# Lead of a fused attention and two-layer MLP kernel: load order, and value-block means by products with value rows as weights

## The chip, the cores and the metric

The kernel runs on one core of one Trainium2 chip. The metric is the device time of one execution in microseconds (us); lower is better. Before the change the median of three runs is 583.91 us (583.61 to 584.04).

## The reference, cut to what matters

Attention over a window of neighbours and over 24 block summaries of 32 positions each (maximum of the keys, mean of the values), then two MLP layers on the 1,536 tokens.

```python
# q, k, v: (B, H, S, D) = (2, 8, 768, 64); block, window = 32, 16; nb = S // block = 24
k_sum = k.reshape(B, H, nb, block, D).max(axis=3)
v_sum = v.reshape(B, H, nb, block, D).mean(axis=3)
scores_l = scale * np.matmul(q, k.transpose(0, 1, 3, 2))          # kept where |i - j| < window
scores_s = scale * np.einsum('bhsd,bhnd->bhsn', q, k_sum) + np.log(block)
a = softmax(concatenate([where(mask_l, scores_l, -1e9), scores_s], -1))
x = matmul(a, concatenate([v, v_sum], axis=2))                    # -> (1536, 512)
h = np.maximum(x @ w_in, 0.0);  x = h * h @ w_out                 # 512 -> 2048 -> 512
h = x @ w_in2;  out = (h * sigmoid(h)) @ w_out2
```

What the change touches is `v_sum` of the first of the two batches, and the order in which the first inputs are fetched.

## The kernel before

**Tiles.** The queries are cut into 24 tiles of 64 positions, 12 per batch. A tile sees 96 keys of its window and 24 block summaries, 120 columns in all. The eight heads are taken as four pairs (`NHP`, "pair 0" to "pair 3"). The first eight tiles are called the lead (`NLEAD`): their attention must be done before the first MLP product can start. The MLP works on blocks of 512 tokens, the first of which is just these eight tiles. TensorE products of the MLP are in fp32r, split into a high and a low part; the products of the attention are in plain fp32.

**Steps of the lead.** The functions inside `first_block` (lines 635 to 840) are named as the planner names them:

- `kt`, `q`, `cst`, `vr`, `vl` (lines 663 to 681) issue loads on SyncE's queue (SP): a pair's keys (384 KB), the queries of four lead tiles (512 KB), mask and identity matrix (244 KB), 256 value rows (512 KB), and the 96 value rows of each of four tiles (768 KB). In the profile these are `t_ksum`, `qrlead`, `cst_sb`, `vrows` and `vlead`.
- `ksum` (VectorE, line 684) takes the maximum over each block of 32 keys; `kwl` (ScalarE, 691) and `ksl` (VectorE, 696) copy windows and maxima of a pair into `kws`, 120 columns for each of four tiles.
- `psl(g, hp)` (TensorE, 698 to 707) makes the scores of tile g for head pair hp: two products of 64 by 64 by 120 (`pss`, four records in the trace). Behind psl(3, 0) and psl(3, 1) it also issues 6 and 4 idle products of 512 columns (`turn`, `FILL`, line 47), which keep TensorE busy; ten more stand at the very start (`WARM`, line 650).
- `ttl` (VectorE, 437) adds the mask and takes the row minimum, `exl` (ScalarE, 444) the exponential; `ze`, `rc`, `nt` (VectorE, 464 to 477) the guard, the inverse and the scaling by it. In the trace these have tile `T` (and `m`, `z`, `r`).
- `psa(g)` (TensorE, 479) transposes a tile's weights, four transposes; `a(g)` (485) copies them out of PSUM, on ScalarE for tiles 0 to 4, on VectorE for tiles 5 to 7.
- `vs(c)` (TensorE, 709 to 711) adds 128 value rows to the 24 block means in `psv`: one fp32 product of 512 columns, with a window of `share` as weights, into rows 96 to 119 of one PSUM bank. `share` holds 1/32 in four of its 88 columns, and the window slides by four with c. The six `vs` accumulate.
- `vmean(i)` (ScalarE, 713) copies the means out of PSUM into the last 24 rows of `vlead`, for four tiles at once.
- `av(g)` (TensorE, 810) multiplies the weights of tiles g and g+1 with `vlead`; `xh` (ScalarE) and `xl` (VectorE) split the result into the high and low part of `xt`, the input of the MLP.
- `sc`, `sh`, `st2`, `hi`, `lo` (753 to 770) decode and split a chunk of MLP weights: `sc` and `hi` on ScalarE, the others on VectorE.
- `highs(0)` (772) is the first MLP product; it needs all four `xh`. `gemm10` adds the low part of the input, `gemm11` is the next chunk.

```python
        def vs(c):
            lo = NSUM - P // KBLK - c * (P // KBLK)
            mm(psv[NWIN:NK], share[:, lo:lo + NSUM], vrows[c // 2][:, c % 2], start=(c == 0), stop=(c == S // P - 1))
```

**What sets the order.** `first_order()` (lines 70 to 241) is a planner in Python. Each step has an engine, a duration, a due time and the steps it waits for; the planner places them one after another, always the step that can start first on its engine, among those ready by then the one due first. Loads are taken to land one after another at a fixed rate. The result is a fixed sequence, and SP, TensorE, ScalarE and VectorE each execute their steps in exactly that order (`manual_schedule`, line 890). A step that waits holds back everything behind it on its engine. PSUM tiles are shared: all four `psl` of a tile write one bank, and its four `ttl` read it; a step that touches a bank waits for the steps of other engines that touch it and stand ahead of it in the sequence.

Of the kernel before, what the change touches and what calls it, by code (L numbers as in the profile page):

```python
# [10 lines left out]
F32 = mybir.dt.float32  # L11
# [8 lines left out]
B, H, S, D = 2, 8, 768, 64  # L20
# [49 lines left out]
def first_order():  # L70
# [6 lines left out]
    def op(eng, name, arg, dur, due, deps=(), bank=(), kb=0):  # L77
        o = index[name, arg] = dict(eng=eng, name=name, arg=arg, dur=dur, due=due + shift.get(name, 0), deps=list(deps), bank=bank, kb=kb,
                                    n=len(ops))
        ops.append(o)  # L80
# [17 lines left out]
        return 24 + 7 * s  # L98


    for i, (name, arg, kb) in enumerate([("kt", 0, 393), ("q", 0, 524), ("kt", 1, 393), ("cst", 0, 250), ("kt", 2, 393),
                                         ("kt", 3, 393), ("q", 1, 524), ("vr", 0, 524), ("vr", 1, 524), ("vr", 2, 524),
                                         ("vl", 0, 1150), ("vl", 1, 1150)]):
        load(name, arg, kb, -100 + i)
    for hp in range(NHP):
        op("vec", "ksum", hp, 1.0, -50 + hp, [("kt", hp, 0)])
# [1 line left out]
            op("act", "kwl", (hp, i), .5, -50 + hp + 51 * i, [("kt", hp, 0)])  # L108
            op("vec", "ksl", (hp, i), .13, -50 + hp + 48 * i, [("ksum", hp, 0)])
    for c in range(6):  # L110
        op("pe", "vs", c, .92, 2.7 + .1 * c, [("vr", c // 2, 0)])
    for i in range(NLEAD // NGRP):
        op("act", "vmean", i, 1.9, -5, [("vs", c, M) for c in range(6)] + [("vl", i, 0)] * 0)
    for i in range(NVF):
        op("act", "vfm", i, .6, tile_due(NLEAD) - 10 + i, [("vmean", 0, 0), ("xh", LEADX[-1], 0)])

# [10 lines left out]
    for g in range(NFIRST):  # L127
        due, two = tile_due(g), g - 2 >= NLEAD
        if g < NLEAD:
            for hp in range(NHP):  # L130
                op("pe", "psl", (g, hp), .29, due, [("kwl", (hp, g // NGRP), A), ("ksl", (hp, g // NGRP), A), ("q", g // NGRP, 0)] +
                   [("psl", (g, hp - 1), 0)] * (hp > 0), bank=[] if hp else [("acc", "ttl", (g, NHP - 1))])
                op("vec", "ttl", (g, hp), .21, due, [("psl", (g, hp), M), ("cst", 0, 0)])
                op("act", "exl", (g, hp), .385, due, [("ttl", (g, hp), A)])
            exp = [("exl", (g, hp), A) for hp in range(NHP)]
        else:
            load("kw", g, 246, due - 9, [pss(g - 2) + (M,)] * two)
            load("qr", g, 131, due - 8.9, [("qd", g - 2, A)] * two)
            load("vf", g, 196, due - 6, [av(g - 2) + (M,)] * two)
            op("vec", "kwc", g, .13, due - .5, [("kw", g, 0)] + [("kvr", 2 * NHP - 1, 0)] * (g >= TPB))  # L140
            if TPB <= g < TPB + NVF:
                op("vec", "vfc", g, .35, due, [("vf", g, 0), ("vendc", 0, A)])
            op("pool", "qd", g, .72, due - 5, [("qr", g, .1)] + [pss(g - 2) + (M,)] * two)
            if g == NLEAD:
                op("pe", "vis", g, 1.95, due, [("gemm1", 1, 0), ("kwc", g, A), ("qd", g, A)], bank=[("att", "ttr", g, g + 1)])
            elif g % 2 == 0:
                op("pe", "vis", g, 3.1, due, values(g - 2) + values(g - 1) + [("kwc", g, A), ("qd", g, A)],
                   bank=[("h", "xl", g - 2), ("att", "ttr", g, g + 1)])
            else:
                index["vis", g - 1]["deps"] += [("kwc", g, A), ("qd", g, A)]  # L150
            op("vec", "ttr", g, .84, due, [pss(g) + (M,)] + [psa(g - 2) + (M,)] * two)
            op("act", "exp", g, 1.54, due, [("ttr", g, -.45)])
            exp = [("exp", g, A)]
        op("vec", "ze", g, .09, due, exp)
        op("vec", "rc", g, .1, due, [("ze", g, .1)])
        op("vec", "nt", g, .78, due, [("rc", g, .1)])
        if g < NLEAD:
            op("pe", "psa", g, .62, due - 2, [("nt", g, -.1)], bank=[("att", "a", g)])
        elif g % 2 == 0:
            op("pe", "psa", g, .85, due - 2, [("nt", g, -.1)], bank=[("att", "a", g, g + 1)])  # L160
        else:
            index["psa", g - 1]["deps"] += [("nt", g, -.1)]
        op("vec" if g in AVEC else "act", "a", g, .65 if g in AVEC else .56, due, [psa(g) + (M,)] + [av(g - 2) + (M,)] * (g >= NLEAD + 2))
        if g < NLEAD and g % 2:
            op("pe", "av", g - 1, 1.15, due, [("vl", g // NGRP, 0), ("vmean", g // NGRP, A), ("a", g - 1, A), ("a", g, A)],
               bank=[("acc", "xl", g - 1)])
            op("act", "xh", g - 1, .6, due, [("av", g - 1, M)])
            op("vec", "xl", g - 1, .7, due, [("xh", g - 1, A)])
        elif g % 2:
            if g == NFIRST - 1:  # L170
                op("pe", "av", g - 1, 1.3, due, values(g - 1) + values(g), bank=[("h", "xl", g - 1)])
            op("act", "xh", g - 1, .6, due, [av(g) + (M - 1.8 * (g < NFIRST - 1),)])
            op("vec", "xl", g - 1, .7, due, [("xh", g - 1, A)])
# [71 lines left out]
def kernel(  # L245
# [32 lines left out]
    def mm(o, l, r, **kw):  # L278
        pe.matmul(o, l, r, **kw)  # L279

    def copy(eng, o, i, scale=1.0):
        if eng is act:
            return act.activation(out=o, in_=i, func=AF.Copy, scale=scale)  # L283
        return eng.tensor_copy(out=o, in_=i)  # L284
# [88 lines left out]


    share_p = ctx.enter_context(tc.tile_pool(name="share_p", bufs=1, side="right"))
    share = share_p.tile([P, PHASE - 8], F32, tag="share", name="share")
    att_ctx = ExitStack()
    cp = att_ctx.enter_context(tc.tile_pool(name="cp", bufs=1, side="right"))
    p1 = att_ctx.enter_context(tc.tile_pool(name="p1", bufs=1, side="right"))
# [14 lines left out]

    pool.memset(share, 0.0)
    for j in range(P // KBLK):
        pool.memset(share[j * KBLK:(j + 1) * KBLK, NSUM - P // KBLK + j:NSUM - P // KBLK + j + 1], 1.0 / KBLK)
    st = {}

    def summaries(b, sums, tag):  # L400
# [234 lines left out]
    def first_block():  # L635
# [3 lines left out]

        idle_in = wi_p.tile([P, 512], F32R, tag="wi", name="idle_in")  # L640
        idle_out = ps_h.tile([P, 512], F32, tag="h", name="idle_out")
        psv = ps_h.tile([P, DM], F32, tag="h", name="psv0")
        vec.memset(idle_in.bitcast(F32), 0.0)
        early = first_p.tile([P, 1], F32, tag="early", name="early")
        act.activation(out=early, in_=idle_in[:, 0:1].bitcast(F32), func=AF.Exp)
# [18 lines left out]
            sp.dma_start(out=kts[hp][:, WIN:], in_=kT[0, hp])  # L664

        def q(i):
            gr = slice(i * NGRP, i * NGRP + NGRP)
            sp.dma_start(out=qrlead[i], in_=qW[gr].rearrange("g e d n -> (e d) g n"))

        def cst_(_):  # L670
            sp.dma_start(out=cst_sb[:, 0:3 * NK + P], in_=cst)
# [35 lines left out]
            turn(FILL.get(ghp, 0))  # L707

        def vs(c):
            lo = NSUM - P // KBLK - c * (P // KBLK)  # L710
            mm(psv[NWIN:NK], share[:, lo:lo + NSUM], vrows[c // 2][:, c % 2], start=(c == 0), stop=(c == S // P - 1))

        def vmean(i):
            means = psv[NWIN:NK]
            copy(act, vlead[NWIN:NK, i * NGRP:i * NGRP + NGRP].rearrange("p g h d -> p g (h d)"),
                 bass.AP(means.tensor, means.offset, [means.ap[0], [0, NGRP], means.ap[1]]))

# [101 lines left out]
        def psa(g):  # L819
            for i in (g,) if g < NLEAD else (g, g + 1):  # L820
                transposes(i)

        do = dict(kt=kt, q=q, cst=cst_, vr=vr, vl=vl, ksum=ksum_, kwl=kwl, ksl=ksl, vs=vs, vmean=vmean, vfm=vfm, kv=kv, kvr=kvr,
                  vend=vend, vendc=vendc, vfc=vfc, kw=kw_load, qr=q_load, vf=v_load, kwc=k_sums, qd=side_by_side,
                  vis=vis, ttr=minima, exp=exps, ze=guard, rc=inverse, psl=psl, ttl=lambda a: minimum(*a),
                  exl=lambda a: exponential(*a), nt=lambda g: norm(g, vec),
# [393 lines left out]
```

## Time and profile before

| what | us |
|---|---|
| median of three runs | 583.91 (583.61 to 584.04) |
| the profiled execution: its own time | 583.73 |
| the profiled execution: its span | 581.9 |
| TensorE busy in the span | 574.5 |
| VectorE busy | 386.4 |
| ScalarE busy | 360.1 |
| start of the first MLP product (highs) | 34.91 |

The span runs from the first to the last instruction; the execution's own time includes what lies around it. PE is TensorE's products, PEld its weight loads, DVE is VectorE, ACT is ScalarE, SPq the issue of loads. Most TensorE products go through the helper `mm` and so stand at line 279, copies at 283 and 284: the tile's name tells them apart. An fp32 product appears as two records, each with a weight load of its own.

### The profile page before, as it was taken

What the parts mean: (1) busy time and instruction counts of PE and PEld (TensorE: products, weight loads), DVE (VectorE), ACT (ScalarE), POOL (GpSimd) and SP (SyncE); (2) the same over time, 40 slices, a digit from 0 to 9 for tenths busy, and PEclk for the clock granted to TensorE, in tenths of its full rate; (3) what the DMA queues carried; (4) which work ended last, traced back from release to release, by engine and by line L of the source; (5) the groups of instructions that cost most, each with busy time, mean ns of one, the idle gap of its engine ahead of it and who ended that gap; (6) DMA issues with size and microseconds to landing.
All of it is one profiled execution on the core that took longest, in us unless ns stands there. A gap on an engine that the chain in (4) does not pass through costs nothing.

```text
span 581.9 us, 9507 instructions
## 1 busy us (share of the span) xinstructions
PE 574.5 (99%) x3300; PEld 489.5 (84%) x3300; DVE 386.4 (66%) x966; ACT 360.1 (62%) x834; POOL 93.0 (16%) x101
## 2 busy tenths in 40 slices
PE   8999999999999999999999999999999999999997
PEld 6578888888888888888888889999988988889995
DVE  5999899953955765286454778666665666666641
ACT  5999878864646545376544677565555655555541
POOL 0010100102654452175332200000000000000000
PEclk9999999999999999999999999999999999999999
DMA  8999989755998879345880111242258411111002
GB/s 317 310 267 330 316 296 333 241 212 168 295 339 289 298 245 364 122 134 160 313 262 2 38 54 73 90 146 90 91 169 338 146 37 37 36 37 37 27 12 108
DMA packets 42240, 104.42 MB, mean 179 GB/s; under 512 B 4560, under 2 KB 11856, under 8 KB 42192
## 3 DMA queue, kind: packets, MB, share of 16 engines
q1 hardware_dynamic: 42192, 103.81, 52.7%
q8 instruction: 26, 0.43, 0.3%
q14 instruction: 22, 0.18, 0.1%
HBM read 78.37 MB, written 25.43 MB: 178 GB/s over the span
## 4 chain that ended last, share of the span: by engine, by line
PE 96%; ACT 2%; DMA 1%; DVE 1%; SPq 0%; issue 0%; DVEq 0%
PE acc L279 45%; PE h L279 23%; PE hx L279 12%; PE hz L279 6%; PE pss L279 3%; PE hy L279 3%; PE psa L483 2%; PE av L279 1%; DMA t_ksum<-in_kT_dram 1%; PE psv L279 1%; ACT vlead L283 1%; ACT T L446 0%; ACT xt L283 0%; PE idle_out L279 0%; DVE ksum L684 0%; DVE T L441 0%
## 5 line engine op out<-in xcount | busy, mean ns | idle before, releaser
L279 PE MATMUL h<-xt,wi 128*128 128x512 f32 x576 | 139.8, 392 | 1.0 <-ACT xt L283 1.0
L279 PE MATMUL acc<-g,wo 128*128 128x512 f32 x576 | 139.5, 391 | 0.0
L279 PE MATMUL acc<-wq,g 128*128 128x512 f32 x576 | 134.3, 390 | 0.0
L279 PEld LDWEIGHTS h<-xt,wi 128*128 128x128 f32 x576 | 107.1, 188 | 23.9 <-ACT xt L283 1.1
L279 PEld LDWEIGHTS acc<-g,wo 128*128 128x128 f32 x576 | 107.6, 188 | 22.6 <-issue 0.5
L279 PEld LDWEIGHTS acc<-wq,g 128*128 128x128 f32 x576 | 107.8, 188 | 21.9 <-DVE wq L287 0.3
L287 DVE TENSOR_TENSOR g<-r,g 128x512 fp32r<-128x512 f32 x48 | 38.8, 807 | 66.0 <-ACT g L283 40.1
L287 DVE TENSOR_TENSOR r_s<-v,r_s 128x256 fp32r<-128x256 f32 x48 | 20.3, 426 | 64.7 <-ACT r_s L283 64.7
L283 ACT ACTIVATE e<-hx 128x384 f32<-128x384 f32 x32 | 15.7, 492 | 60.4 <-PE hx L279 60.4
L446 ACT ACTIVATE T<-T,m 128x120 f32<-128x120 f32 x96 | 36.6, 382 | 7.0 <-DVE m L441 6.9
L283 ACT ACTIVATE g<-s 128x384 fp32r<-128x384 f32 x64 | 32.9, 516 | 10.5 <-DVE s L287 10.4
L279 PE MATMUL hx<-x_t,r_s 128*128 128x384 f32 x192 | 38.5, 335 | 0.0
L287 DVE TENSOR_TENSOR g<-s,g 128x384 fp32r<-128x384 f32 x64 | 35.3, 555 | 2.7 <-ACT g L283 1.1
L279 PEld LDWEIGHTS hx<-x_t,r_s 128*128 128x128 f32 x192 | 33.8, 188 | 0.3
L1032 ACT ACTIVATE s<-e 128x384 f32<-128x384 f32 x48 | 25.1, 523 | 8.4 <-DVE e L287 7.1
L284 POOL COPY qd<-qr 128x256 f32<-128x256 f32 x16 | 12.0, 767 | 111.0 <-PE pss L279 68.2
L287 POOL TENSOR_TENSOR wo<-c_wo,wo 128x512 fp32r<-128x512 f32 x16 | 25.9, 1619 | 19.2 <-ACT wo L283 18.7
L588 ACT ACTIVATE r<-h 128x512 f32<-128x512 f32 x16 | 9.6, 597 | 30.9 <-PE h L279 30.9
L592 ACT ACTIVATE r<-h 128x512 f32<-128x512 f32 x16 | 9.5, 593 | 30.6 <-PE h L279 30.6
L287 DVE TENSOR_TENSOR s<-e,s 128x384 f32<-128x384 f32 x48 | 26.4, 551 | 0.3 <-ACT s L1032 0.3
L287 POOL TENSOR_TENSOR r<-r 128x512 f32<-128x512 f32 x16 | 16.6, 1040 | 49.3 <-ACT g L593 38.1
L477 DVE TENSOR_SCALAR T<-T,r 128x120 f32<-128x120 f32 x96 | 24.2, 316 | 0.5
(112 smaller groups left out, 905.8 us busy)
## 6 DMA issues: line engine op xcount, KB each, us to landing
raw_wi<-in_w_in_dram SPq DMA_DIRECT2D x16, 512.0 KB, 5.0
raw_wo<-in_w_out_dram SPq DMA_DIRECT2D x16, 512.0 KB, 5.4
raw_wp<-in_w_out_dram SPq DMA_DIRECT2D x16, 512.0 KB, 4.9
split<-wo SPq DMA_DIRECT2D x16, 512.0 KB, 3.8
raw_wj<-in_w_in_dram SPq DMA_DIRECT2D x16, 512.0 KB, 4.7
wo<-split SPq DMA_DIRECT2D x16, 512.0 KB, 3.6
c<-scr_dram SPq DMA_DIRECT2D x32, 256.0 KB, 2.8
scr_dram<-c_wo SPq DMA_DIRECT2D x16, 256.0 KB, 3.7
```

The source lines that it names most:

```text
L279: pe.matmul(o, l, r, **kw)
L283: return act.activation(out=o, in_=i, func=AF.Copy, scale=scale)
L284: return eng.tensor_copy(out=o, in_=i)
L287: return eng.tensor_tensor(out=o, in0=a, in1=b, op=op)
L446: act.activation(out=d["T"][:, c], in_=d["T"][:, c], func=AF.Exp, bias=d["m"][:, c:c + 1], scale=-1.0, accum_out=d["z"][:, c:c + 1])
L477: st["norm"] = vec.tensor_scalar(out=T[:, c], in0=T[:, c], scalar1=r[:, c:c + 1], scalar2=None, op0=ALU.mult)
L483: pe.transpose(ps[0:NK, c], d["T"][:, c], id_sb)
L588: act.activation(out=r, in_=h, func=AF.Relu)
L592: act.activation(out=r, in_=h, func=AF.Relu)
L1032: act.activation(out=s, in_=src, func=AF.Sigmoid)
```

## The change

- The loads are reordered: mask and identity become the third load. The queries come in four loads of two tiles (256 KB each) instead of two of four tiles; `psl(g, hp)` waits for load `g // 2`. The last query load stands behind the first MLP weight chunk, which the planner now places ahead of both `vl`.
- `share` keeps only four columns (1/32 where row block and column agree). `vs(c)` is now four fp32 products: 128 value rows by 128 channels as weights, `share`'s four columns as the moving operand. Each yields four block means, channels on the partitions, in its own columns of `psv`; nothing is accumulated.
- `vsc` (VectorE) copies these 96 columns to `vsumT`, and `vst` (TensorE) turns them with four fp32 products, `vsumT` as weights and the identity as moving operand, so that the means stand in rows 96 to 119 as before. `vmean` reads that tile.
- The planner gets new durations and due times for these steps, and so a new order for the whole lead.

```diff
--- before.py
+++ after.py
@@ -98,9 +98,9 @@
         return 24 + 7 * s
 
 
-    for i, (name, arg, kb) in enumerate([("kt", 0, 393), ("q", 0, 524), ("kt", 1, 393), ("cst", 0, 250), ("kt", 2, 393),
-                                         ("kt", 3, 393), ("q", 1, 524), ("vr", 0, 524), ("vr", 1, 524), ("vr", 2, 524),
-                                         ("vl", 0, 1150), ("vl", 1, 1150)]):
+    for i, (name, arg, kb) in enumerate([("kt", 0, 393), ("q", 0, 262), ("cst", 0, 250), ("kt", 1, 393), ("q", 1, 262),
+                                         ("kt", 2, 393), ("kt", 3, 393), ("q", 2, 262), ("vr", 0, 524), ("vr", 1, 524),
+                                         ("vr", 2, 524), ("q", 3, 262), ("vl", 0, 1150), ("vl", 1, 1150)]):
         load(name, arg, kb, -100 + i)
     for hp in range(NHP):
         op("vec", "ksum", hp, 1.0, -50 + hp, [("kt", hp, 0)])
@@ -108,9 +108,11 @@
             op("act", "kwl", (hp, i), .5, -50 + hp + 51 * i, [("kt", hp, 0)])
             op("vec", "ksl", (hp, i), .13, -50 + hp + 48 * i, [("ksum", hp, 0)])
     for c in range(6):
-        op("pe", "vs", c, .92, 2.7 + .1 * c, [("vr", c // 2, 0)])
-    for i in range(NLEAD // NGRP):
-        op("act", "vmean", i, 1.9, -5, [("vs", c, M) for c in range(6)] + [("vl", i, 0)] * 0)
+        op("pe", "vs", c, .47, 1.4 + .1 * c, [("vr", c // 2, 0)])
+    op("vec", "vsc", 0, .3, 1.4, [("vs", c, M) for c in range(6)])
+    op("pe", "vst", 0, .9, -4, [("vsc", 0, A)])
+    op("act", "vmean", 0, 1.9, 1.4, [("vst", 0, M)])
+    op("act", "vmean", 1, 1.9, 1.9, [("vst", 0, M)])
     for i in range(NVF):
         op("act", "vfm", i, .6, tile_due(NLEAD) - 10 + i, [("vmean", 0, 0), ("xh", LEADX[-1], 0)])
 
@@ -128,7 +130,7 @@
         due, two = tile_due(g), g - 2 >= NLEAD
         if g < NLEAD:
             for hp in range(NHP):
-                op("pe", "psl", (g, hp), .29, due, [("kwl", (hp, g // NGRP), A), ("ksl", (hp, g // NGRP), A), ("q", g // NGRP, 0)] +
+                op("pe", "psl", (g, hp), .29, due, [("kwl", (hp, g // NGRP), A), ("ksl", (hp, g // NGRP), A), ("q", g // 2, 0)] +
                    [("psl", (g, hp - 1), 0)] * (hp > 0), bank=[] if hp else [("acc", "ttl", (g, NHP - 1))])
                 op("vec", "ttl", (g, hp), .21, due, [("psl", (g, hp), M), ("cst", 0, 0)])
                 op("act", "exl", (g, hp), .385, due, [("ttl", (g, hp), A)])
@@ -373,7 +375,7 @@
 
 
     share_p = ctx.enter_context(tc.tile_pool(name="share_p", bufs=1, side="right"))
-    share = share_p.tile([P, PHASE - 8], F32, tag="share", name="share")
+    share = share_p.tile([P, PHASE - 8], F32, tag="share", name="share")[:, 0:P // KBLK]
     att_ctx = ExitStack()
     cp = att_ctx.enter_context(tc.tile_pool(name="cp", bufs=1, side="right"))
     p1 = att_ctx.enter_context(tc.tile_pool(name="p1", bufs=1, side="right"))
@@ -394,7 +396,7 @@
 
     pool.memset(share, 0.0)
     for j in range(P // KBLK):
-        pool.memset(share[j * KBLK:(j + 1) * KBLK, NSUM - P // KBLK + j:NSUM - P // KBLK + j + 1], 1.0 / KBLK)
+        pool.memset(share[j * KBLK:(j + 1) * KBLK, j:j + 1], 1.0 / KBLK)
     st = {}
 
     def summaries(b, sums, tag):
@@ -639,7 +641,7 @@
 
         idle_in = wi_p.tile([P, 512], F32R, tag="wi", name="idle_in")
         idle_out = ps_h.tile([P, 512], F32, tag="h", name="idle_out")
-        psv = ps_h.tile([P, DM], F32, tag="h", name="psv0")
+        psv = ps_h.tile([P, NHP, NSUM], F32, tag="h", name="psv0")
         vec.memset(idle_in.bitcast(F32), 0.0)
         early = first_p.tile([P, 1], F32, tag="early", name="early")
         act.activation(out=early, in_=idle_in[:, 0:1].bitcast(F32), func=AF.Exp)
@@ -664,8 +666,8 @@
             sp.dma_start(out=kts[hp][:, WIN:], in_=kT[0, hp])
 
         def q(i):
-            gr = slice(i * NGRP, i * NGRP + NGRP)
-            sp.dma_start(out=qrlead[i], in_=qW[gr].rearrange("g e d n -> (e d) g n"))
+            lo = 2 * i % NGRP
+            sp.dma_start(out=qrlead[2 * i // NGRP][:, lo:lo + 2], in_=qW[2 * i:2 * i + 2].rearrange("g e d n -> (e d) g n"))
 
         def cst_(_):
             sp.dma_start(out=cst_sb[:, 0:3 * NK + P], in_=cst)
@@ -707,11 +709,21 @@
             turn(FILL.get(ghp, 0))
 
         def vs(c):
-            lo = NSUM - P // KBLK - c * (P // KBLK)
-            mm(psv[NWIN:NK], share[:, lo:lo + NSUM], vrows[c // 2][:, c % 2], start=(c == 0), stop=(c == S // P - 1))
+            n = P // KBLK
+            for hp in range(NHP):
+                mm(psv[:, hp, c * n:(c + 1) * n], vrows[c // 2][:, c % 2, hp * P:(hp + 1) * P], share, start=True, stop=True)
+
+        def vsc(_):
+            vsumT[0] = first_p.tile([P, NHP, NSUM], F32, tag="vsumT0", name="vsumT0")
+            copy(vec, vsumT[0], psv)
+
+        def vst(_):
+            ps = st["vst"] = ps_h.tile([P, NHP, P], F32, tag="h", name="pst0")
+            for hp in range(NHP):
+                mm(ps[NWIN:NK, hp], vsumT[0][:, hp], id_sb, start=True, stop=True)
 
         def vmean(i):
-            means = psv[NWIN:NK]
+            means = st["vst"][NWIN:NK].rearrange("p c d -> p (c d)")
             copy(act, vlead[NWIN:NK, i * NGRP:i * NGRP + NGRP].rearrange("p g h d -> p g (h d)"),
                  bass.AP(means.tensor, means.offset, [means.ap[0], [0, NGRP], means.ap[1]]))
 
@@ -820,7 +832,7 @@
             for i in (g,) if g < NLEAD else (g, g + 1):
                 transposes(i)
 
-        do = dict(kt=kt, q=q, cst=cst_, vr=vr, vl=vl, ksum=ksum_, kwl=kwl, ksl=ksl, vs=vs, vmean=vmean, vfm=vfm, kv=kv, kvr=kvr,
+        do = dict(kt=kt, q=q, cst=cst_, vr=vr, vl=vl, ksum=ksum_, kwl=kwl, ksl=ksl, vs=vs, vsc=vsc, vst=vst, vmean=vmean, vfm=vfm, kv=kv, kvr=kvr,
                   vend=vend, vendc=vendc, vfc=vfc, kw=kw_load, qr=q_load, vf=v_load, kwc=k_sums, qd=side_by_side,
                   vis=vis, ttr=minima, exp=exps, ze=guard, rc=inverse, psl=psl, ttl=lambda a: minimum(*a),
                   exl=lambda a: exponential(*a), nt=lambda g: norm(g, vec),
```

## Rows read from the trace of the kernel before

**Rows 1.** The page, busy time by engine: us (share of the span) xinstructions.

```profile
PE 574.5 (99%) x3300; PEld 489.5 (84%) x3300; DVE 386.4 (66%) x966; ACT 360.1 (62%) x834; POOL 93.0 (16%) x101
```

**Rows 2.** Time by stretches: length, busy us of each engine, granted clock, DMA share, GB/s.

```profile
11.83:27.93 16.10, 15.93 (x133) 9.81 (x133) 15.41 (x103) 15.04 (x64) 0.00 (x0) 1.00 1.05 315
27.93:34.91 6.98, 5.42 (x138) 4.77 (x137) 5.73 (x16) 6.85 (x9) 1.27 (x2) 1.00 0.99 301
34.91:581.90 546.99, 543.16 (x2980) 467.85 (x2980) 359.54 (x829) 332.03 (x745) 90.77 (x86) 1.00 0.50 171
```

**Rows 3.** Chain of waits in order of time: start us, us, what.

```profile
17.93 0.91 PE pss L279 x12
...
20.92 0.43 PE pss L279 x4
21.35 1.83 PE psv L279 x4
23.18 0.58 PE psa L483 x4
...
25.31 2.70 PE psv L279 x6
...
33.86 0.51 ACT wi L283
...
34.91 5.74 PE h L279 x24
```

**Rows 4.** Timeline of ScalarE: start us, us, instruction [idle before it <-releaser].

```profile
27.29 0.38 ACT L446 ACTIVATE T<-T,m 128x120 f32<-128x120 f32 x1
...
28.04 3.63 ACT L283 ACTIVATE vlead<-psv 24x2048 f32<-24x2048 f32 x2 [0.28 <-PE psv L279]
```

**Rows 5.** Timeline of SP's queue: issue us, us, instruction.

```profile
1.18 0.42 SPq L668 DMA_DIRECT2D qrlead<-in_qW_dram  x1
...
2.19 0.43 SPq L671 DMA_DIRECT2D cst_sb<-in_cst_dram  x1
```

**Rows 6.** Loads issued from 1.15 and from 2.17 us: KB each, us to landing.

```profile
qrlead<-in_qW_dram SPq DMA_DIRECT2D x1, 512.0 KB, 4.1
...
cst_sb<-in_cst_dram SPq DMA_DIRECT2D x1, 244.0 KB, 6.0
```

**Rows 7.** Timeline of VectorE.

```profile
8.74 0.28 DVE L441 CUSTOM_DVE_ANT_0 T<-pss,cst_sb 128x120 f32<-128x120 f32 x1
...
9.71 0.28 DVE L441 CUSTOM_DVE_ANT_0 T<-pss,cst_sb 128x120 f32<-128x120 f32 x1 [0.28 <-PE pss L279]
...
12.33 0.21 DVE L284 COPY kws<-ksum 128x96 f32<-128x96 f32 x1
12.46 0.28 DVE L441 CUSTOM_DVE_ANT_0 T<-pss,cst_sb 128x120 f32<-128x120 f32 x1
```

**Rows 8.** Timeline of TensorE's products.

```profile
1.46 4.63 PE L279 MATMUL idle_out<-idle_in 128*128 128x512 f32 x10 [1.46 <-DVE idle_in L643]
...
9.17 1.59 PE L279 MATMUL pss<-kws,qrlead 64*64 64x120 f32 x16 [0.28 <-DVE m L441]
10.69 1.21 PE L279 MATMUL idle_out<-idle_in 128*128 128x512 f32 x4
11.83 4.03 PE L279 MATMUL pss<-kws,qrlead 64*64 64x120 f32 x60
```

**Rows 9.** Groups of weight loads by shape: count | busy us, mean ns | idle before.

```profile
L279 PEld LDWEIGHTS h<-xt,wi 128*128 128x128 f32 x576 | 107.1, 188 | 23.9 <-ACT xt L283 1.1 <-issue 0.8
...
L279 PEld LDWEIGHTS av<-a,vlead 120*64 120x64 f32 x128 | 3.8, 138 | 0.5 <-ACT vlead L283 0.5
L279 PEld LDWEIGHTS psv<-vrows,share 128*24 128x24 f32 x12 | 1.0, 102 | 2.4 <-issue 2.3
```

**Rows 10.** Timeline of weight loads, windows 108.5 to 109.2 and 29.9 to 30.2 us.

```profile
108.96 0.30 PEld L279 LDWEIGHTS h<-xt,wi 128*128 128x128 f32 x2
...
29.96 0.37 PEld L279 LDWEIGHTS av<-a,vlead 120*64 120x64 f32 x10 [0.50 <-ACT vlead L283]
```

## The prediction, made before the changed kernel ran

> **What bounds the kernel now.** I read the page's first part, then the time by stretches. TensorE is busy in 99% of the span [rows 1]. From 34.91 us to the end it works 543.16 of 546.99 us at the full granted clock, so a shift of that stage's start stays to the end; the lead before it has gaps [rows 2]. The change lies wholly in the lead. The chain of waits there ends with the value sums on TensorE (2.70 us from 25.31), the vmean copies on ScalarE, four xh with an sc and a hi between them, and highs at 34.91 [rows 3]. vmean begins when the last vs product is out, and ScalarE had been idle for only 0.28 us before it [rows 4]: TensorE and ScalarE both bound the lead, TensorE by a hair. So I work out when the means stand in PSUM after the change, and what ScalarE has to do from there.
>
> **The order after the change.** With the new entries the planner issues on TensorE: psl of pair 0 for tiles 0 to 3, the six idle products, psl of pair 1 and the four idle ones, pairs 2 and 3, tiles 4 and 5, and towards the end of these psa0, psl(5,3), vs0, psa1, vs1, psa2, vs2, psa3, psl of tile 6, vs3, psl of tile 7, vs4, vs5, psa4, vst, psa5, psa6, av0. On ScalarE vmean0 comes behind exl(7,0), vmean1 behind exl(7,3), and hi of w_in chunk 1 goes from before xh6 to behind it. On VectorE vsc stands between rc5 and nt5.
>
> **Loads.** q(1), the queries of tiles 2 and 3, now lands behind 384+256+244+384+256 = 1,524 KB. The mask load of before had the same 1,524 KB up to its end, and landed at 2.19+6.0 = 8.2 us [rows 5, 6]. The mask now lands behind 884 KB, near where 896 KB had landed (1.18+4.1 = 5.3 us) [rows 5, 6], so ttl(0,0) and ttl(1,0) run some 2 us before 8.74 [rows 7]. That alone gains nothing, because of the next term. The other moves in SP's queue are covered: at the 315 GB/s of this stretch [rows 2] the last value rows, the weight chunk and the third and fourth quarter of the queries land at some 16.5, 18, 11.5 and 19 us (estimates), and their users come at 26, 20.5, 15 and 23 us. The two extra issues of 0.43 us on SP [rows 5] lie under transfers already queued. vl comes some 2 us later and is read near 32. Up to the second vl the bytes are the same, so what follows lands as before. POOL's memsets keep their number, and its next work waits on loads after 30 us. Tiles 0 and 1 gain nothing from their smaller load: the ten warming products, 4.63 us from 1.46, hold TensorE until 6.0 [rows 8].
>
> **Term 1, the idle products stand behind q(1).** TensorE takes its instructions in order. psl(2,0) waits for q(1) until 8.15, two psl of 0.24 follow, then six idle products. Four of them took 1.14 us up to the next psl (10.69 to 11.83) [rows 8] and each more takes 0.24 (24 of the same width in 5.74) [rows 3], so 1.62. psl(0,1) starts at 10.3 instead of 9.17. ttl(0,1) came 0.54 behind it with the wait before the product, and comes some 0.45 behind without: 10.73 instead of 9.71 [rows 7, 8]. It stands ahead of ksum2 on VectorE, although the third key block has landed at some 9.1. From there to ttl(0,2) VectorE has the same work as before, 2.75 us (9.71 to 12.46, a ttl changing places) [rows 7]. psl(0,3) writes a PSUM tile that ttl(0,2) reads and waits for it, as psl(0,1) waited for VectorE [rows 8]. **+1.0 us.**
>
> **Term 2, TensorE from psl(0,3) to the means.** A psl costs 0.24 (a block of 12 records less one of 4, over two products), entering a block of another kind some 0.15, a psa 0.58 with its entry, an old vs 0.86 (two passes of 0.43) [rows 3].
> A new vs has four products of two weight loads each, 128 columns wide, and streams four columns. No row shows that shape. A load takes 102 ns at 24 columns, 138 at 64 and 188 at 128, that is 0.83 ns a column [rows 9]; two 128-column loads with nothing between them took 0.30 us together, so the second began 0.11 after the first [rows 10]. Eight loads at 0.11 are 0.88 us: as much as the old vs. The cheap bound is av's loads, of which two of 64 columns side by side pass every 0.058 us (ten in 0.37, less 0.138 for the last, over four steps) [rows 9, 10]: 0.47 a vs. The dear bound is the transposes' 0.145 for a load and its product [rows 3]: 1.16. I take 0.88, since the two wide loads are the row of the same width.
> vst streams 128 columns in two passes four times; a pass of 512 took 0.43, so eight of 0.107 are 0.86. Against the old order: vst +0.86, six vs at +0.02 +0.12, one more change of kind +0.15, psa5 now behind the means −0.44, and some 0.16 more of waits of psl(2,3) and psl(4,3) for a ttl in the same PSUM tile. **+0.85 us**; 6 × 0.41 less at the cheap bound, 6 × 0.28 more at the dear one.
> vsc (96 columns, about 0.2 us; a ksl of that width takes 0.13 [rows 7]) waits for vs5, for about 1.4 us, and nt5, ttl(7,1) and the work on tiles 6 and 7 are queued behind it. psa5 waits for nt5, but it is behind vst anyway; exl(7,1) waits for ttl(7,1), and ScalarE is then in vmean0. vsc's own hop is hidden under psa4. With cheap sums these waits are the next to bind.
>
> **Term 3, ScalarE from the means to highs.** Before: 6.98 us, 27.93 to 34.91 [rows 2]. After: vmean0 and vmean1 as before, three exl that now come behind vmean0, 3 × 0.38 = 1.14 [rows 4], four xh, one sc; hi (0.51 [rows 3]) is out of the way, and xh6 waits some 0.27 for a7 and av6, because tile 7's exponentials are later. **+1.14 − 0.51 + 0.27 = +0.90 us.** hi and lo of chunk 1 now run beside highs and the products after it: ScalarE has sc, vfm and hi (1.7 us) and VectorE xl6, st2, sh and lo (about 2.5) before TensorE wants the chunk 2.85 us after highs starts. Covered with about 0.3 to spare; without cover at most hi's 0.51 is lost.
>
> **Sum.** 1.0 + 0.85 + 0.90 = +2.8 us, highs at 37.7 instead of 34.91. The profiled execution took 583.73 us, its span 581.9; the median of the three runs is 583.91, 0.18 above it. So 586.5 on that execution and 586.7 as a median. About 0.2%, 1.17 us, is what a measurement here can tell.
>
> **Rivals.**
> *Short products are cheap (not slower).* If narrow products' loads overlap as av's do, or better, TensorE saves 2.5 us: at 0.47 a vs the sum is 2.8 − 2.5 = +0.3, 584.2 us; at 0.2 a vs TensorE stops being the bound, vsc's queue and the exponentials take over, and by the same chains the sum is −0.4, 583.5 us. For it: av's pairs in 0.058 us [rows 10]. Against it: a load's time grows with its columns, and the wide ones stood 0.11 apart [rows 9, 10]. It decides at 0.86 a vs, below which the six sums shrink. Only if q(1) also lands by 6.6 is it a measurable gain (0.3 less 1.6 of stall: −1.3, 582.6). Chance 0.22.
> The Trainium skill (TensorE: Matmul & The Clock Gate, section Back-to-back issue gap) gives a floor of about 25 ns for a matmul of up to 64 columns; eight such are 0.2 us a vs, and the sum by it is the −0.4 above. No row here has so short a stream, and the rows of wide loads speak against it.
> *q(1) lands early.* With small loads ahead it might come by 6.6; then psl(2,0) hardly waits, the idle products end when psl(0,1) may start anyway, and 1.6 us of stall are gone: +1.2, 585.1 us. For it: transfers run side by side. Against: the mask with the same bytes took until 8.2 [rows 5, 6]. Chance 0.08.
> *The clock falls (slower still).* TensorE idles 1.6 us before q(1) and later streams four columns at a time. The first ten idle products took 0.46 each [rows 8] where later ones took 0.24 [rows 3], the lower and the higher level. If the lower one held through the sums, psl and psa would take twice as long: about +2.2 more, 588.9 us. Against: the clock stayed at 1.00 with 1.56 us of gaps in 6.98 [rows 2]. Chance 0.06.
>
> **Numbers.** Forecast 0.64 (585.6 at 0.7 a vs to 588.4 at 1.16), cheap products 0.22, early q(1) 0.08, clock 0.06. Slower by over 0.2%: the forecast less 0.02, half of the early q(1), the clock and 0.00 of the cheap case: 0.62 + 0.04 + 0.06 = 0.72. Faster: the part of the cheap case with an earlier q(1), 0.08. Within 0.2%: the rest, 0.2. The range goes from 583.5, the cheap case at 0.2 a vs, to 588.4, the dear bound; it leaves out the gains beyond and the clock.
>
> **What would show it.** Right: psl(2,0) near 8.1 and psl(0,1) near 10.3; loads of vrows 0.11 apart, a vs of about 0.9; VectorE idle before vsc; vmean0 near 30; highs near 37.7, and the stage after it as long as now. Wrong: loads of vrows under 0.08 apart, q(1) before 7, or psa and psl at double time.

## The result, and the profile after

The changed kernel takes **588.62 us** (588.50 to 588.81, 4 runs), the kernel before 583.80 (583.61 to 584.04, 4 runs) in the same comparison: ratio 1.0083 [1.0065, 1.0100], 4.8 us slower. The forecast was 586.7 with a range to 588.4. The sign was right; the size was too small by 1.9 us, and the time lies 0.2 above the range.

The profiled execution takes 588.60 us with a span of 586.8. Its page, busy time by engine and then the granted TensorE clock in 40 slices of the span:

```profile
PE 578.1 (99%) x3344; PEld 496.7 (85%) x3344; DVE 385.5 (66%) x967; ACT 360.8 (61%) x834; POOL 94.6 (16%) x101
```

```profile
PEclk8989999999999999999999999999999999999999
```

Against [rows 1], TensorE is busy 3.6 us longer with 44 more records, and two early slices do not have the full clock. The time by stretches says where they lie (length, busy us of PE, PEld, DVE, ACT, POOL, granted clock, DMA share, GB/s):

```profile
5.00:8.50 3.50, 1.84 (x15) 1.22 (x15) 1.55 (x7) 1.57 (x6) 0.00 (x0) 1.00 0.96 348
9.00:12.00 3.00, 3.00 (x10) 1.96 (x12) 0.25 (x3) 1.28 (x5) 0.00 (x0) 0.50 1.06 393
13.00:29.00 16.00, 15.52 (x166) 13.95 (x165) 13.56 (x89) 13.86 (x57) 0.00 (x0) 1.00 1.05 318
29.50:32.50 3.00, 3.00 (x15) 1.97 (x14) 2.09 (x15) 1.65 (x4) 0.35 (x1) 0.50 1.10 256
33.00:39.69 6.69, 5.26 (x135) 4.47 (x133) 5.67 (x17) 6.61 (x14) 0.40 (x1) 1.00 0.33 103
39.69:586.80 547.11, 543.42 (x2980) 468.03 (x2980) 359.26 (x831) 332.51 (x746) 92.48 (x86) 1.00 0.51 171
```

The last row answers to the last one of [rows 2]: 543.42 us busy of 547.11 against 543.16 of 546.99. The stage behind the lead is as long as it was, so the whole loss is in the lead: highs starts at 39.69 instead of 34.91, 4.78 us later. And in the lead the clock is twice at 0.50, the lower level (1.2 of 2.4 GHz), while TensorE is busy in every moment of those stretches. Before, the granted clock was 1.00 from 11.83 on [rows 2].

The chain of waits (start us, us, what) shows what stands there:

```profile
2.63 5.50 DMA qrlead<-in_qW_dram
...
8.17 0.74 PE pss L281 x8
8.91 2.86 PE idle_out L281 x6
11.77 0.63 PE pss L281 x4
...
12.43 0.28 DVE T L443
...
21.50 0.79 PE psv L281 x8
22.29 0.49 PE psa L485 x4
...
27.34 1.88 PE psv L281 x16
29.22 0.72 PE psa L485 x4
29.95 1.85 PE pst L281 x8
...
31.82 1.87 ACT vlead L285
...
33.71 1.25 ACT T L448 x6
...
34.98 1.87 ACT vlead L285
...
39.69 5.75 PE h L281 x24
```

The second query load is on the chain now, and the six idle products behind it take 2.86 us where the forecast had 1.62 for them. The timeline of TensorE's products says what went ahead of them (start us, us, instruction, idle before it):

```profile
5.78 0.74 PE L281 MATMUL pss<-kws,qrlead 64*64 64x120 f32 x8
8.17 0.74 PE L281 MATMUL pss<-kws,qrlead 64*64 64x120 f32 x8 [1.66 <-DMA qrlead<-in_qW_dram]
8.84 2.93 PE L281 MATMUL idle_out<-idle_in 128*128 128x512 f32 x6
```

TensorE stood still for 1.66 us until the load was in. It then ran the products of two tiles at the pace of before (0.74 us for eight records), and from 8.9 us on the idle products at half the clock. The second time it had not stood still: before the clock fell at 29.3 it had gone through the last two of the new value sums. What sets the time of such a sum is its weight loads (TensorE's weight loads in order of time):

```profile
21.23 0.97 PEld L281 LDWEIGHTS psv<-share,vrows 128*128 128x128 f32 x8
22.04 0.50 PEld L485 LDWEIGHTS psa<-cst_sb,T 128*120 128x120 f32 x4
```

Eight loads in 0.97, the last of them 0.19 long (the group's mean is 191 ns): (0.97 − 0.19) / 7 = 0.111 apart, as forecast. The timeline of VectorE has the wait that was forecast ahead of vsc:

```profile
29.26 0.26 DVE L286 COPY vsumT<-psv 128x96 f32<-128x96 f32 x1 [1.24 <-PE psv L281]
```

### The profile page after: what moved, and what is told of

Its sections match the earlier page's. It is cut to its first block, busy times and chain, and to the rows that moved or that the text cites. A ratio compares the mean times of both kernels' runs of the same rounds, so it can differ in the third digit from the quotient of the medians.

```text
span 586.8 us, 9596 instructions
## 1 busy us (share of the span) xinstructions
PE 578.1 (99%) x3344; PEld 496.7 (85%) x3344; DVE 385.5 (66%) x967; ACT 360.8 (61%) x834; POOL 94.6 (16%) x101
## 4 chain that ended last, share of the span: by engine, by line
PE 96%; ACT 1%; DMA 1%; DVE 1%; SPq 0%; issue 0%; DVEq 0%
PE acc L281 45%; PE h L281 23%; PE hx L281 11%; PE hz L281 6%; PE pss L281 3%; PE hy L281 3%; PE psa L485 2%; PE av L281 1%; DMA qrlead<-in_qW_dram 1%; PE psv L281 1%; ACT vlead L285 1%; PE idle_out L281 0%; ACT xt L285 0%; PE pst L281 0%; DVE ksum L686 0%; DVE T L443 0%
## 5 line engine op out<-in xcount | busy, mean ns | idle before, releaser
L443 DVE CUSTOM_DVE_ANT_0 T<-pss,cst_sb 128x120 f32<-128x120 f32 x96 | 21.6, 276 | 6.9 <-PE pss L281 6.8
```

The lines of the kernel that those rows point to most:

```text
L443: vec.tensor_tensor_reduce(out=d["T"][:, c], in0=d["ps"][:, c], in1=cst_sb[:, kind * NK:kind * NK + NK], scale=-0.125, scalar=3.0e38, op0= ...
```

## The experiments

**The theories.** *Clock*: the two falls of the clock are worth about half of the loss, and the second one comes because the new products stream four columns behind two wide weight loads, so that TensorE's array does little although TensorE is busy. *Stall*: most of the loss is the idle products behind the late query load, at either clock. *Dear sums*: the new sums cost TensorE and the tail what the chain shows, whatever the clock is. Every kernel here computes all of the reference; only idle products are moved or left out. The times are medians beside runs of the kernel before on the same chip (584.08 to 584.13).

### One half of the change at a time

**New loads, old sums.** The diff against the changed kernel is its second and third bullet taken back:

```diff
-        op("pe", "vs", c, .47, 1.4 + .1 * c, [("vr", c // 2, 0)])
-    op("vec", "vsc", 0, .3, 1.4, [("vs", c, M) for c in range(6)])
...
+        op("pe", "vs", c, .92, 2.7 + .1 * c, [("vr", c // 2, 0)])
...
+            mm(psv[NWIN:NK], share[:, lo:lo + NSUM], vrows[c // 2][:, c % 2], start=(c == 0), stop=(c == S // P - 1))
```

> New load order with the old value sums (one 512-column product each, accumulated; no vsc, no vst; the planner orders the rest). Theory: the cost has two separate sources, the idle products behind the late query load (with the fall of the clock that the wait brings on) and the new sums (with a second fall, brought on by their short streams). Then the first fall near 8.9 us stays, the second near 29 is gone, and highs starts at 36.8 to 37.6: +1.9 to +2.7 us against before, 585.7 to 586.5. Rival 1, the sums are the whole cost and the load order is harmless: within 0.4 of before, 583.4 to 584.2. Rival 2, the second fall is only the first one's echo (TensorE late and idle): a second fall shows here too, and some 587.5.

Measured: 585.93 us (584.37 to 587.08, 10 runs), ratio 1.0028 [1.0016, 1.0040]. The ten runs are of two kinds: five with a mean clock of 0.997 take 586.4 to 587.1, five with 0.999 or 1.000 take 584.4 to 585.5. The profiled one (584.41) is among the three shortest, has no fall, and its load was in at 7.4:

```profile
7.44 0.74 PE L279 MATMUL pss<-kws,qrlead 64*64 64x120 f32 x8 [1.17 <-DMA qrlead<-in_qW_dram]
8.11 1.67 PE L279 MATMUL idle_out<-idle_in 128*128 128x512 f32 x6
```

The same six products take 1.67 us here and 2.93 in the changed kernel. With the clock held the stall alone puts highs at 35.55, 0.64 late. In this profile there was no fall late in the lead either.

**Old loads, new sums.**

```diff
-    for i, (name, arg, kb) in enumerate([("kt", 0, 393), ("q", 0, 262), ("cst", 0, 250), ("kt", 1, 393), ("q", 1, 262),
...
+    for i, (name, arg, kb) in enumerate([("kt", 0, 393), ("q", 0, 524), ("kt", 1, 393), ("cst", 0, 250), ("kt", 2, 393),
...
```

> Old load order with the new value sums. Theory: no wait near 6.5 to 8.1 and no fall near 8.9, idle products done by 9 us; the sums' loads and vst alone put highs at 36.4 to 36.9 (+1.5 to +2.0, 585.4), and a fall of the clock among or behind the sums makes it 37.8 to 38.4 (+3.0 to +3.5, 587.0). Rival 1, the sums are the whole cost: +4.8, as in the full change. Rival 2, the late fall is an echo of the early one: no fall here, +1.5 to +2.0.

Measured: 589.91 us (588.70 to 590.62, 4 runs), 1.0094 [1.0079, 1.0109]: this half alone loses at least as much as the whole change, and more than was expected of it: 5.8 us above the kernel before, and the loads alone 1.8, where both together lose 4.8. There is no early fall and no stall. The late fall came sooner and lasted through the last two sums, vst and the transposes (a stretch as above, then two steps of the timeline of weight loads):

```profile
26.00:32.00 6.00, 5.90 (x27) 4.83 (x28) 3.60 (x14) 2.01 (x9) 0.00 (x0) 0.50 1.05 365
```

```profile
21.42 1.86 PEld L281 LDWEIGHTS psv<-share,vrows 128*128 128x128 f32 x16
...
25.50 3.39 PEld L281 LDWEIGHTS psv<-share,vrows 128*128 128x128 f32 x16
```

Sixteen equal weight loads take 1.86 us before the fall and 3.39 in it. Highs starts at 39.67. So the late fall comes with the new sums and without the new loads; here it lasted longer than in the changed kernel, and the two halves do not add up to the whole.

### Without the stall

**Six idle products earlier.** They stand behind psl(1, 0), ahead of the products that wait for the load; the order of everything else is the changed kernel's.

```diff
-FILL = {(NGRP - 1, 0): 6, (NGRP - 1, 1): 4}
+FILL = {(1, 0): 6, (NGRP - 1, 1): 4}
```

> The changed kernel with the six idle products behind psl(1,0), where TensorE waits for the queries, in place of psl(3,0); the order is otherwise the same. Theory: no fall near 8.9, psl(0,1) starts near 9 instead of 11.7, everything up to the sums is 2.5 to 3 us earlier, and the late fall, owed to the sums, stays: highs at 36.3 to 37.2, +1.4 to +2.3 against before, 585.2 to 586.1. If the late fall goes too: highs near 35.3, +0.4, 584.2. Rival 1 (the load order is harmless because something else bounds there): no gain over the changed kernel, 588.6.

Measured: 590.11 us (584.79 to 590.64, 10 runs), 1.0074 [1.0047, 1.0101], above the 585.2 to 586.1 expected, and not one time but three: two runs at 584.8 with a clock of 0.999, two at 586.0 and 586.5, six at 590.05 to 590.64 with 0.986 to 0.988. The order is the same in all; what differs is the clock, by some 5.5 us. The profiled run is one without a fall, and so shows what the new sums cost at full clock (chain of waits):

```profile
18.82 0.79 PE psv L281 x8
19.61 0.49 PE psa L485 x4
20.10 0.79 PE psv L281 x8
...
24.67 1.88 PE psv L281 x16
26.55 0.51 PE psa L485 x4
...
27.07 0.60 ACT a L285
27.67 0.37 ACT T L448 x2
...
28.07 1.87 ACT vlead L285
...
29.96 1.24 ACT T L448 x6
...
35.94 4.15 PE h L281 x17
```

The first vmean starts at 28.07, where it started at 28.04 before [rows 4], and highs 7.87 us behind it instead of 6.87: the new sums cost TensorE nothing, and the tail 1.0. The chain now comes to vmean through ScalarE's own queue (a and two exl), but that queue had stood waiting for psa4, which stands behind the last two sums (timeline of ScalarE):

```profile
27.07 0.60 ACT L285 ACTIVATE a<-psa 120x512 f32<-120x512 f32 x1 [1.14 <-PE psa L485]
```

So the sums are still on the chain, and cheaper ones would have brought vmean forward; by how much, no run shows.

**The same with the old sums.** The two edits above together.

> New load order, old value sums, six idle products behind psl(1,0). Theory: no fall of the clock at all, psl(0,1) near 9, and highs at 33.9 to 34.4: 0.5 to 1.0 us less than before, 582.9 to 583.4. Rival 1 (sums are the whole cost, loads harmless): as before, 583.8.

Measured: 583.74 us (583.39 to 584.31, 10 runs), 0.9990 [0.9980, 0.9999], all clocks 0.999 or 1.000, the first vmean at 28.06 and highs at 34.92. The idle products behind the wait, with the lower clock in half of those runs, were what the new loads cost (585.93 to 583.74), but the time expected, at most 583.4, was not reached: against the kernel before the gain is 0.4 us, and highs starts where it did. The load was in at 8.41 in this profile, and the products behind it start at 8.46, later than the early mask would let them.

**No idle products in the lead** (`FILL = {}`).

> The changed kernel without the ten idle products behind psl(3,0) and psl(3,1). Theory: the stall behind the late queries is the idle products; without them psl(0,1) starts near 8.9, and the chains alone give highs near 35.7 where the clock holds (+0.8, 584.6) and 37 to 38 where it falls (+2 to +3, 586 to 587); with less streamed the falls should be at least as frequent. Rival (the wait itself is the cost, the idle products are free): psl(0,1) no earlier than 10, 588.6.

Measured: 590.03 us (586.33 to 590.99, 8 runs), 1.0080 [1.0056, 1.0103], every clock 0.982 to 0.993, and more than any time that was expected. The stall is gone and nothing is won: the clock falls in two stretches that are longer than the changed kernel's, from an idle wait of 2.18 us and from the sums. Highs starts at 41.96 in the profiled execution, which took 590.81.

```profile
9.00:14.00 5.00, 4.61 (x48) 4.17 (x46) 4.39 (x23) 4.16 (x16) 0.00 (x0) 0.50 1.07 394
...
22.00:35.00 13.00, 13.00 (x75) 11.05 (x74) 6.49 (x40) 6.40 (x24) 1.23 (x2) 0.50 1.04 338
```

### The same sums with wider streams

Here each new product streams 64 columns instead of four: the sliding window of `share` comes back, 64 wide, the products of a pair accumulate into 64 columns of `psv`, and vsc copies the first 24 of them. Weight loads, number of products and order are those of the changed kernel.

```diff
-                mm(psv[:, hp, c * n:(c + 1) * n], vrows[c // 2][:, c % 2, hp * P:(hp + 1) * P], share, start=True, stop=True)
+                mm(psv[:, hp], vrows[c // 2][:, c % 2, hp * P:(hp + 1) * P], share[:, lo:lo + 64], start=c == hp == 0,
+                   stop=c == S // P - 1, skip_group_check=True)
...
-            copy(vec, vsumT[0], psv)
+            copy(vec, vsumT[0], psv[:, :, 0:NSUM])
```

**With the idle products earlier:**

> The kernel with the six idle products behind psl(1,0), and each value-sum product now streams 64 columns (60 of them zeros in the sliding window of the mask, accumulated) where it streamed 4. The weight loads, two of 128 columns a product at 0.10 us each, take longer than 64 columns in a pass (0.053), so TensorE's time for the sums should not change. Theory: the late fall of the clock comes because TensorE streams almost nothing while it loads; with sixteen times the columns it stays away, and all executions lie at 584.8 plus or minus 0.4, without the 590.2 that most executions of the narrow form took. Rival: the fall comes from the lead's gaps and waits whatever the products stream: the spread stays, 584.8 to 590.6. Rival 2: the wide form is dearer, a pass and a load do not overlap: 6 x 0.4 us more, 587.2.

Measured: **584.78 us** (584.25 to 585.76, 10 runs), 1.0013 [1.0003, 1.0022], every clock 0.999 or 1.000, against 590.11 with four columns. The stretch from 16 to 28 us, first with 64 columns, then with four (the run without a fall):

```profile
16.00:28.00 12.00, 12.00 (x116) 10.81 (x115) 9.57 (x65) 9.66 (x38) 0.00 (x0) 1.00 1.04 313
```

```profile
16.00:28.00 12.00, 12.00 (x119) 10.77 (x116) 9.68 (x66) 9.72 (x39) 0.00 (x0) 1.00 1.05 278
```

TensorE is busy for all of it in both, with the same weight loads, and from one sum to the next are 1.28 us in both (18.21 to 19.49 with 64 columns, 18.82 to 20.10 with four). What differs is what the products stream. Sixteen times as many columns cost no time and keep the clock in ten runs of ten: that the late fall hangs on the narrow streams is shown. (The two forms ran on different chips, each beside the kernel before; on the chip of the wide one the narrow form without idle products lost the clock in eight runs of eight, and its profile has the late fall.)

**With the idle products where the change has them:**

> The changed kernel with the 64-column sums and nothing else altered (idle products where the change has them). Theory: the late fall near 29 us goes, the early one near 8.9, owed to the wait for the queries, stays in the executions that have it: 586.0 to 587.4 (588.6 less 1.3 to 2.5), highs near 37.2 to 38.4. Rival (the falls do not hang on the streamed columns): 588.6 as the full change.

Measured: 586.43 us (585.71 to 587.46, 5 runs), 1.0039 [1.0026, 1.0053]: 2.3 us above the kernel before beside it, where the change lost 4.8. In the profiled run TensorE went on at 7.40 and no fall followed; one run of five has a clock of 0.997, and it is the longest. So the early fall is gone from most of these runs too, which the streams that come after it cannot explain, and the 2.5 us between the two kernels hold both falls. What the narrow streams cost alone is read from the pair above.

**With the old loads:**

> Old load order with the new value sums in their 64-column form: what the new sums cost when the clock holds. Theory: no fall; the turning products and three exponentials behind the first vmean remain: highs at 36.2 to 36.9, +1.3 to +2.0, 585.4 to 586.1. Rival (the new sums are free but for the clock): within 0.4 of before, 583.7 to 584.5. Rival 2 (64 columns do not hold the clock with this order): 587 and more, as the narrow form's 588.7 to 590.6.

Measured: 586.49 us (585.99 to 586.89, 5 runs), 1.0040 [1.0026, 1.0054], against 589.91 with four columns. It is more than expected: at full clock the new sums still cost 2.4 us here. VectorE (timeline) and the chain of waits say why:

```profile
27.75 0.26 DVE L286 COPY vsumT<-psv 128x96 f32<-128x96 f32 x1 [0.80 <-PE psv L281]
27.92 0.68 DVE L336 SCALAR_TENSOR_TENSOR c_wi<-c_wi,raw_wi 128x512 int32<-128x512 int32 x1
```

```profile
27.92 0.69 DVE c_wi L336
...
28.64 0.63 ACT wi L285
...
29.29 1.87 ACT vlead L285
```

VectorE stands in vsc's wait; st2 of a weight chunk is queued behind it, ScalarE's hi waits for st2, and vmean is queued behind hi. The first vmean so starts at 29.29, 1.25 later than before, behind a step that has nothing to do with the means.

### Both early query loads first

**Old sums, loads in the order keys 0, queries 0, queries 1, mask, keys 1:** the reordering without the load that comes late, and with the idle products where they were.

```diff
-    for i, (name, arg, kb) in enumerate([("kt", 0, 393), ("q", 0, 262), ("cst", 0, 250), ("kt", 1, 393), ("q", 1, 262),
+    for i, (name, arg, kb) in enumerate([("kt", 0, 393), ("q", 0, 262), ("q", 1, 262), ("cst", 0, 250), ("kt", 1, 393),
```

> Old value sums; loads in the order keys 0, queries of tiles 0 and 1, queries of tiles 2 and 3, mask, keys 1, and the rest as in the change; idle products where they were. Theory: no wait before the idle products, so no stall and no fall; four ttl run before ksum1 and the lead gains what the early mask was worth: highs near 33.6, -1.2 against before, 582.6 to 583.2. Rival (the early mask is worth nothing because VectorE and ScalarE are bound by the later key blocks): as before, 583.9 to 584.2.

Measured: **583.04 us** (582.70 to 583.57, 10 runs), 0.9982 [0.9973, 0.9992], faster than both kernels, as expected. TensorE goes through the first tiles without a wait, and VectorE's minima come ahead of the second maximum:

```profile
6.02 1.22 PE L279 MATMUL pss<-kws,qrlead 64*64 64x120 f32 x16
```

```profile
7.28 0.28 DVE L441 CUSTOM_DVE_ANT_0 T<-pss,cst_sb 128x120 f32<-128x120 f32 x1
...
7.49 0.95 DVE L684 TENSOR_REDUCE ksum<-t_ksum 128x24 f32<-128x768 f32 x1
```

Highs starts at 34.01, 0.90 earlier than before. vmean starts 1.29 earlier (26.75 against 28.04); 0.4 of that is lost again to a weight chunk's step on VectorE, for which ScalarE waits in the tail.

**The same loads with the new sums, 64 columns wide:**

> All of the change's parts with the two faults mended: both early query loads ahead of the mask, and the new sums in the 64-column form. Theory: no wait, no fall; against the same loads with the old sums (583.0) the new ones still cost the turning and the later exponentials: highs near 35.2, +0.2 to +0.9 against before, 584.0 to 584.9. Rival (the new sums gain once the clock holds): 582.5 or less.

Measured: 584.89 us (584.21 to 586.37, 10 runs), 1.0015 [1.0005, 1.0024], at the upper end of what was expected and 1.85 above the old sums on the same loads. Not all of that belongs to the sums: of the 2.00 us between the two profiles (highs at 36.01 and 34.01) 1.05 stand ahead of any sum. The mask landed 5.4 us after its issue here and 3.8 there, and psl(0,1) starts at 9.88 instead of 8.83. That leaves 0.95 for the new sums at full clock, beside 1.0 on the changed kernel's loads with the earlier idle products and 2.4 on the old loads. They gain nowhere.

## Why the prediction was right and wrong

**What failed** is the third rival, "the clock falls", given 0.06 and left out of the sum and the range; the two falls cost about 2.5 of the 4.8 us (the terms below). It was set aside with [rows 2]: the clock had stayed at 1.00 through 1.56 us of gaps in 6.98. Those gaps were three waits, none longer than 0.99 us, and said nothing of one of 1.66, nor of products that stream four columns. A fall came behind each of the two things that the rival named, the idle wait and the narrow streams; the second alone is worth up to 5.5 us (the runs with earlier idle products). The rival's own price, 588.9, is 0.3 from the time measured, but by luck: the falls took the idle products, psa4 and vst instead of the sums. It had read the lower level from the first ten idle products, 0.46 us each; the granted clock of that stretch reads 1.00 (0 to 6 us of the kernel before), so no row calls it the lower level, though the six idle products in the fall took 0.48 each at 0.50.

**Term 1 (+1.0).** The load was in when forecast: psl(2,0) at 8.17 (forecast 8.15). The six idle products took 2.86 instead of 1.62, and ttl(0,2) came at 15.17 instead of 12.46 [rows 7]: +2.7 (timeline of VectorE).

```profile
15.17 0.28 DVE L443 CUSTOM_DVE_ANT_0 T<-pss,cst_sb 128x120 f32<-128x120 f32 x1
```

What it would be with the clock held can be worked out from the run with old sums, where psl(2,0) at 7.44 gave ttl(0,2) at 13.00, +0.54; 0.73 later makes +1.3. So the mechanism held, the term was 0.3 short by itself, and the fall added 1.4.

**Term 2 (+0.85).** From ttl(0,2) to the first vmean: 15.17 to 31.82, 16.65, against 12.46 to 28.04, 15.58: +1.1, near the forecast, but by luck and for another reason. psa4 took 0.72 and vst 1.90 in the timeline, where the profile with the earlier idle products, which has no fall, shows 0.51 and 1.05 (timeline of TensorE's products):

```profile
26.97 1.05 PE L281 MATMUL pst<-cst_sb,vsumT 128*24 128x128 f32 x8
```

That makes 1.1 for the fall. Without a fall the term is nought: 12.49 to 28.07 in that profile. The spacing of the wide loads was right, 0.111; wrong was that a sum and the transposes behind it cost at least what they had cost before (chain of waits of the kernel before):

```profile
23.76 0.97 PE psv L279 x2
24.73 0.58 PE psa L483 x4
```

These 1.55 us were to grow by 0.02. A new sum that stands behind transposes takes 0.79 and the transposes behind it 0.49, together 1.28 (21.50 to 22.78). Over the six sums and psa1 to psa4 the forecast is 0.7 us too long, most of the term.

**The rival of cheap sums** falls with the same rows: the loads stand 0.111 apart, not 0.058 or less. The Trainium skill (TensorE: Matmul & The Clock Gate, section Back-to-back issue gap) gives about 25 ns for such narrow products, but the same section says that a stream of loads and products is set by both; here the loads set it, and the measurement decides.

**Term 3 (+0.90).** vmean to highs: 31.82 to 39.69, 7.87, against 6.87 before (28.04 to 34.91): +1.0. Three exl stand between the two vmean (1.25 us in the chain), as forecast.

**The waits and the cover.** VectorE idles 1.24 before vsc (forecast 1.4), and in this order it holds up nothing else. That this depends on the order, the run with old loads and wide sums shows. The stage behind highs is as long as before, so hi and lo of chunk 1 were covered. The second query load did not come by 6.6 in any profile of the changed load order: it landed at 7.4 to 8.5 us.

**The sum with the clock held** would be 1.3 + 0.0 + 1.0 = +2.3, forecast +2.8; the two falls added about 1.4 and 1.1, and 4.8 was measured.

**Open** is why the fall lasts from 3 to 13 us in different kernels, and why a run of one kernel falls and the next does not. That an idle wait starts the early fall is argued: the two profiles that show it have waits of 1.66 and 2.18 us, and in the longer one the clock fell at 8.1 us, inside the wait, while three profiles with waits of 0.74, 1.10 and 1.17 us kept 1.00; no run changed that wait alone. Some runs with new loads and old sums at a clock of 1.000 took 585.4 and others 584.4; the landing time of the load (7.4 to 8.5 us in the profiles) may be the cause, but no profile of the longer kind was taken.

## What to carry to other kernels

Replacing one wide product by several narrow ones saves no TensorE time when each needs its own wide weights: count the weight loads, then look at what the stream does to the clock, since a busy TensorE that streams almost nothing can lose half of it. A load moved to the front pushes others back; find the instruction that waits for the one pushed back, and do not leave filler work queued behind that wait. And when an order is planned anew, read what stands behind each new wait on the in-order engines: here a copy of 0.26 us held a weight chunk, and the chunk held the means.

## What the runs showed of the hardware

- The granted clock fell to 0.50 in stretches in which TensorE was busy for 5.90 of 6.00 us, and for 13.00 of 13.00. With the same busy time, the same weight loads and 64 streamed columns instead of four it stayed at 1.00 (590.11 against 584.78 us).
- Weight loads slow down with the clock: sixteen of 128 columns took 1.86 us at 1.00 and 3.39 at 0.50.
- A product of 64 columns costs no more than one of four when each has its own 128-column weights: 1.28 us from one sum to the next in both.
- The same query load, with the same bytes ahead of it and issued at 2.63 us, landed 4.7, 4.8, 5.4, 5.5, 5.7, 5.8 and 5.9 us after its issue in seven profiles. An order that is tight against such a load is tight against the latest of these.
